# Reading two PSUM banks with ScalarE alone, and adding the parts with GpSimd

## The chip, the cores and the metric

The kernel runs on one core of a Trainium2 chip. The metric is the time of one execution on the device in microseconds (us). Five engines work side by side, each through its own queue in order: TensorE (PE; its weight loads are listed as PEld), VectorE (DVE), ScalarE (ACT), GpSimd (POOL) and SyncE (SP), which here issues nearly all DMAs. Matmuls write to PSUM, eight banks of 128 partitions by 512 floats; the other engines copy results from there to SBUF.

## The reference

A gated sum of two branches over an input x of 2048 rows and 640 columns:

```python
g = sigmoid((x * gate_w).sum(-1, keepdims=True))
a = attention(x, wqkv) @ wo          # 32 heads of 20 columns, softmax over 2048 keys
fa = x @ dft_hid_re.T;  fb = x @ dft_hid_im.T          # DFT over the features
b = dft_seq_re @ fa - dft_seq_im @ fb                  # real part of the DFT over the rows
return g * a + (1 - g) * b
```

All of it is in float32. Matmuls that need that precision split each operand into a leading part and a rest and add three products.

## The kernel before

The first 270 us project queries, keys and values, and make 10 of 64 tiles of the feature DFT. From then on the attention runs in 256 *cycles* of four *steps*; step i is one of 1024 pairs of score tiles of the second pass. In each cycle TensorE computes eight score tiles for the row maxima (kind "m", read by VectorE, L170) and eight for the exponentials (kind "e", read by ScalarE, L832), and between them a share of the other branch (kind "F", fill). At the end stands "B", `burst`: 16 matmuls of probabilities and values (L494). The order is written out by hand as a string of 16 scores, the fills and the burst:

```python
ORDER = "emFemFFFFemFeFFmeFFemFFFmmFFmeeB"
```

Cycle c begins the steps 4c+1 to 4c+4, one with every second "e" (`begin(i)`, `end(i)`). `at_step(i, fn)` lets `begin(i)` call `fn`; this sets the place of a DMA in SyncE's queue and of an operation in its engine's queue, while the time follows from semaphores. `extras` holds read-outs and adds with the step from which they may run; `run_extras`, called in `burst` ahead of its matmuls, takes up to two of them.

Score tiles rotate over five PSUM banks (`ps`), the values' sum holds one (`av`), and two banks, `yp0` and `yp1`, take the fill. A fill tile is computed in halves: rows 0 to 63 of both operands go to `yp0`, rows 64 to 127 to `yp1`, and the result is the sum of the two banks. The fills are, in order:

- 54 feature tiles (`hid_tile`, matmuls at L346), one per cycle, until 605 us. Tile c ends with the last fill of cycle c, at step 4c+3; its banks are read at the end of that cycle: ScalarE copies `yp0` to a `raw` buffer with its sign (L354), VectorE adds `yp1` (L355). The store to `a_scr` in HBM is put at step now+2, which is 4c+5.
- the DFT over the rows (`dft_step`, L575), until 1688 us, read in the same way (L594, L595); the change does not touch it.
- 30 output tiles (`out_tile`, L646), one per cycle. ScalarE copies `yp0` times the gate to a tile `m` (L655), VectorE adds `yp1` times the gate (L658). In the last 41 steps VectorE does both (L657, L658). GpSimd scales the other branch's row and adds `m` (L662, L663).

The `raw` buffers (`raw_tile`, three of 128x1024 floats) are shared. In the feature stage they serve each tile, from its read-out until its store has landed, and the loads that are split by GpSimd afterwards: `load_wb` (the next 128x966 and 128x644 weights, in cycles 6 and 22) and `load_c` (two 128x1024 pieces of the row DFT, in cycles 47, 49 and 51; GpSimd adds the two at L465 and splits the sum at L112 and L113). Both take two `raw` buffers when `end(4c+2)` calls them, and are split from step 4c+4 or 4c+6 on. GpSimd also multiplies the attention's output by the reciprocal sums (L524). A tile that takes a buffer waits until the buffer's last user is done with it. SyncE's other transfers in this stage are the queries' and keys' rows of the next pair of heads (L785), the rows of maxima (L210, L211, put two steps behind a `burst`), and the sums' way through HBM (L508 to L532).

Of the kernel before, what the change touches and what calls it, by code (L numbers as in the profile page):

```python
# [10 lines left out]
F32 = mybir.dt.float32  # L11
R = mybir.dt.float32r
AF = mybir.ActivationFunctionType
ALU = mybir.AluOpType
# [4 lines left out]
P = 128  # L19
# [7 lines left out]
HE = D // 2  # L27
# [40 lines left out]
def f32(ap):  # L68
    return ap.bitcast(F32)
# [3 lines left out]
def mix_kernel(ctx: ExitStack, tc: tile.TileContext, xa, wqk, wb, cdft, wo, out):  # L73
    nc = tc.nc
    pe, act, dve, pool, sp = nc.tensor, nc.scalar, nc.vector, nc.gpsimd, nc.sync
# [15 lines left out]
    a_scr = dram.tile([2, 2, NS, P, HE], F32, name="a_scr")  # L91
# [36 lines left out]
    def raw_tile():  # L128
        return work.tile([P, 1024], F32, name="raw", bufs=3)
# [22 lines left out]
    now, later = [-1], {}  # L152

    def at_step(i, fn):
        later.setdefault(i, []).append(fn)
# [38 lines left out]
    def new_y(z):  # L194
        yp[z] = ps_y.tile([P, 512], F32, name=f"yp{z}")
        return yp[z]
# [139 lines left out]
    def hid_tile(i, read_out):  # L336
        j, st = divmod(i, NS)
        hf, ri = divmod(j, 2)
        new_y(0), new_y(1)
        w = wt["b", 2 + j]  # L340
        cs = slice(st * P, (st + 1) * P)
        for d in range(ND):
            for z, (xz, wz) in enumerate(((0, 0), (0, 1), (1, 0))):
                for h in range(2):
                    r = slice(64 * h, 64 * h + 64)
                    pe.matmul(yp[h][:, :HE], xs[r, xz, d, cs], w[r, wz, d, :HE],  # L346
                              start=d == 0 and z == 0, stop=d == ND - 1 and z == 2)
                if (d, z) != (ND - 1, 2):
                    yield
        a = raw_tile()[:, :HE]  # L350
        y0, y1 = yp[0][:, :HE], yp[1][:, :HE]

        def read():
            act.activation(a, y0, AF.Copy, scale=-1.0 if ri else 1.0)  # L354
            dve.tensor_tensor(a, a, y1, op=ALU.subtract if ri else ALU.add)  # L355

        read_out(read, (a_scr[ri, hf, st], a))
        yield


    def segment(i, steps):
        def read_out(read, args):
            read()
            stores.append(args)

        tile_ = hid_tile(i, read_out)
        left = 3 * ND
        for k in range(steps):
            run_s(step + 1)
            for _ in range(left // (steps - k)):  # L370
                next(tile_)
                left -= 1
# [3 lines left out]
    def run_s(upto):  # L376
        nonlocal step
        while step < upto:
            s_step(step)
            step += 1  # L380
# [37 lines left out]
    for n, c in enumerate(order):  # L418
        for t in range(4):
            m = 4 * n + t  # L420
# [24 lines left out]
    def a_tile(n, s):  # L445
        at[n, s] = apool[0].tile([P, 2, HE], R, name=f"a{n}_{s}")
        return at[n, s]
# [97 lines left out]
    st = {(th * HT + t, hf): 0 for th in range(2) for t in range(HT) for hf in range(2)}  # L545
# [4 lines left out]
    outs, extras, made = {}, [], {}  # L550
# [83 lines left out]
    def out_tile(tt, hf):  # L634
        new_y(0), new_y(1)
        if hf == 0:
            k = tt - PRE[0]
            yo[tt] = f32(a_tile(1, 2 * ND + k) if 2 * ND + k < NS else a_tile(0, k)).rearrange("p z c -> p (z c)")
            assert all(st[tt, h] == 0 for h in range(2))
            sp.dma_start(yo[tt], y_scr[tt])  # L640
        o = opre[tt]
        for d in range(ND - 1):
            for z, (oz, wz) in enumerate(((0, 0), (0, 1), (1, 0))):
                for h in range(2):
                    r = slice(64 * h, 64 * h + 64)
                    pe.matmul(yp[h][:, :HE], o[r, oz, d], wos[d, hf][r, wz], start=d == 0 and z == 0, stop=d == ND - 2 and z == 2)  # L646
                if (d, z) != (ND - 2, 2):
                    yield
        m = apool[0].tile([P, HE], F32, name="m", bufs=2)
        y0, y1 = yp[0][:, :HE], yp[1][:, :HE]  # L650
        g = gate[:, tt : tt + 1]

        def read():
            if now[0] < total - LEAD:
                act.activation(m, y0, AF.Copy, scale=g)  # L655
            else:
                dve.tensor_scalar(m, y0, g, 1.0, op0=ALU.mult, op1=ALU.mult)  # L657
            dve.scalar_tensor_tensor(m, y1, g, m, op0=ALU.mult, op1=ALU.add)  # L658

        def add():  # L660
            y = yo[tt][:, hf * HE : (hf + 1) * HE]
            pool.tensor_scalar(y, y, ngate[:, tt : tt + 1], float(signs[tt, hf]), op0=ALU.mult, op1=ALU.mult)  # L662
            pool.tensor_tensor(y, y, m, op=ALU.add)  # L663

        extras.append((now[0], read))
        extras.append((now[0] + 3, add))
        yield

# [33 lines left out]
    apool = []  # L702
# [28 lines left out]
    LAST = {total - 10: load_o4, total - 9: load_old, total - 8: lambda: fins.append(load_o(0)), total - 2: lambda: fins.pop()()}  # L731
    done = 0
    goals, fins = {}, []
    def read_later(read, args):
        extras.append((now[0], read))
        at_step(now[0] + 2, functools.partial(sp.dma_start, *args))

    HID = 4 * NS - HEAD
    fills = itertools.chain(*(hid_tile(HEAD + g, read_later) for g in range(HID)), itertools.chain.from_iterable(dft_step(g) for g in range(NS * UNITS)),
                            itertools.chain.from_iterable(out_tile(tt, hf) for tt in PRE for hf in range(2)))  # L740


# [238 lines left out]
```

## Time and profile before

| | |
|---|---|
| time, median of 3 runs | 1891.77 us (1891.42 to 1894.12) |
| span of the profiled execution, first to last instruction | 1888.5 us |
| the execution's own time beside its span | not shown by the profile; the runs' median is 3.3 us above the span |
| granted TensorE clock, mean | 1.000 |
| HBM traffic over the span | 147 GB/s |
| TensorE: row DFT (L575), feature DFT (L346), output (L646) matmuls | 649.1, 236.0, 89.5 us |
| VectorE: maxima (L170) | 1294.8 us, 2048 of 684 ns |
| ScalarE: exponentials (L832) | 1087.0 us, 2048 of 599 ns |

A row of a group or a waiting list gives engine, line, operation, result and operands, and the count; a timeline row begins with the start and the duration in us, and ends, in brackets, with the time that the engine had been idle and what released it. A row of a window gives the busy time of PE, PEld, DVE, ACT and POOL in it with the number of instructions, the granted clock, the DMA engines' busy share and the GB/s moved.

### The profile page before, as it was taken

To read this page: it belongs to the slowest core of one execution; us is meant where nothing else is said; L and a number is where in the kernel's file an instruction comes from. 1 tells how busy PE (TensorE), PEld (TensorE's weight loads), DVE (VectorE), ACT (ScalarE), POOL (GpSimd) and SP (SyncE) were. 2 spreads that over 40 slices of the span, in tenths; PEclk is the share of its full clock that TensorE was granted. 3 is DMA by queue.
4 is the path that set the end of the run, shared out by engine and by line. 5 is a ranking of instruction groups with operands and counts; after the bars stand their busy time and mean duration, and the time that the engine had idled before them with its cause. 6 is when DMAs were issued, how large, how long until landed. Compare 5 with 4: busy or idle time off the path is not lost. (4 is left out here: it accounts for less than half of the span.)

```text
span 1888.5 us, 44537 instructions
## 1 busy us (share of the span) xinstructions
PE 1877.4 (99%) x17453; PEld 1358.2 (72%) x17453; DVE 1470.0 (78%) x2445; ACT 1219.1 (65%) x2350; POOL 1005.1 (53%) x872
## 2 busy tenths in 40 slices
PE   9999999999999999999999999999999999999998
PEld 8987777777776677776767677776767677766666
DVE  4145569989898888888888888888888888889954
ACT  4221147777777767666767667666767676677785
POOL 1200001010004999466699989958879988734343
PEclk9999999999999999999999999999999999999999
DMA  7843341221215575536557576736475746442214
GB/s 232 181 133 128 128 154 48 62 76 49 75 58 147 163 238 178 148 123 169 180 176 238 171 234 190 201 119 189 156 220 195 225 147 205 154 114 70 62 49 157
DMA packets 174804, 280.50 MB, mean 149 GB/s; under 512 B 44303, under 2 KB 106895, under 8 KB 174595
## 3 DMA queue, kind: packets, MB, share of 16 engines
q1 hardware_dynamic: 173635, 275.70, 47.7%
q0 software_dynamic: 960, 1.97, 0.6%
q8 instruction: 137, 2.24, 0.5%
q14 instruction: 72, 0.59, 0.1%
HBM read 213.37 MB, written 63.52 MB: 147 GB/s over the span
## 5 line engine op out<-in xcount | busy, mean ns | idle before, releaser
L170 DVE TENSOR_REDUCE mx<-ps 128x1 f32<-128x512 f32 x2048 | 1294.8, 684 | 175.8 <-PE ps L168 154.8
L832 ACT ACTIVATE p<-ps 128x512 f32<-128x512 f32 x2048 | 1087.0, 599 | 432.7 <-PE ps L168 223.6
L168 PE MATMUL ps<-kst,qst 60*128 60x512 f32 x2048 | 785.2, 415 | 3.7 <-DVE mx L170 1.7
L830 PE MATMUL ps<-qst,kst 62*128 62x512 f32 x2048 | 698.9, 413 | 0.5 <-ACT p L832 0.3
L575 PE MATMUL yp<-a,part 64*128 64x320 f32 x5376 | 649.1, 307 | 0.0
L575 PEld LDWEIGHTS yp<-a,part 64*128 64x128 f32 x5376 | 582.2, 186 | 7.3
L494 PE MATMUL av<-p,v 128*21 128x512 f32 x4096 | 491.3, 596 | 0.0
L830 PEld LDWEIGHTS ps<-qst,kst 62*128 62x128 f32 x2048 | 335.7, 185 | 200.9 <-DVE mx L170 182.4
L168 PEld LDWEIGHTS ps<-kst,qst 60*128 60x128 f32 x2048 | 371.2, 184 | 24.7 <-DVE mx L170 9.6
L113 POOL TENSOR_TENSOR part<-raw,part 128x1024 fp32r<-128x1024 f32 (+1 forms) x129 | 290.4, 2251 | 10.3
L494 PEld LDWEIGHTS av<-p,v 128*21 128x21 f32 x4096 | 98.4, 100 | 226.7 <-issue 223.2
L346 PE MATMUL yp<-wb,xs 64*128 64x320 f32 x1920 | 236.0, 308 | 0.1
L112 POOL CAST part<-raw 128x1024 fp32r<-128x1024 f32 (+1 forms) x129 | 127.0, 985 | 161.5 <-PE yp L575 141.2
L346 PEld LDWEIGHTS yp<-wb,xs 64*128 64x128 f32 x1920 | 206.0, 186 | 4.5 <-DVE raw L355 0.5
L465 POOL TENSOR_TENSOR raw<-raw,raw 128x1024 f32<-128x1024 f32 x77 | 185.4, 2408 | 6.4 <-DMA raw<-in_cdft 4.8
L112 POOL CAST wb<-raw 128x966 fp32r<-128x966 f32 (+1 forms) x4 | 3.4, 862 | 255.4 <-DMA raw<-in_wb 255.4
L524 POOL TENSOR_TENSOR o<-o,rb 128x512 f32<-128x512 f32 x31 | 40.2, 1296 | 146.6 <-DMA rb<-r_scr 100.8
L113 POOL TENSOR_TENSOR a<-araw,a 128x320 fp32r<-128x320 f32 x112 | 97.6, 872 | 9.0
L113 DVE TENSOR_TENSOR p<-ps,p 128x512 fp32r<-128x512 f32 x40 | 27.5, 691 | 93.5 <-ACT p L110 90.8
L646 PE MATMUL yp<-a,part 64*128 64x320 f32 x720 | 89.5, 309 | 0.0
L110 ACT ACTIVATE p<-ps 128x512 fp32r<-128x512 f32 x40 | 23.7, 597 | 100.6 <-PE ps L118 100.6
L646 PEld LDWEIGHTS yp<-a,part 64*128 64x128 f32 x720 | 76.9, 186 | 2.5
(86 smaller groups left out, 1237.0 us busy)
## 6 DMA issues: line engine op xcount, KB each, us to landing
raw<-in_cdft SPq DMA_DIRECT2D x192, 512.0 KB
araw<-a_scr SPq DMA_DIRECT2D x192, 160.0 KB
qk_scr<-p SPq DMA_DIRECT2D x40, 512.0 KB
kst<-qk_scr SPq DMA_DIRECT2D x90, 160.0 KB
qst<-qk_scr SPq DMA_DIRECT2D x90, 160.0 KB
a_scr<-raw SPq DMA_DIRECT2D x64, 160.0 KB
yt<-y_scr SPq DMA_DIRECT2D x64, 160.0 KB
y_scr<-yt SPq DMA_DIRECT2D x64, 160.0 KB
```

What stands on the lines that cost most here:

```text
L112: e1.tensor_copy(dst1, src)
L113: e2.tensor_tensor(dst2, src, f32(dst1), op=ALU.subtract)
L168: pe.matmul(ps, q[b : b + KROWS, qt * P : (qt + 1) * P], k[b : b + KROWS, kc * 512 : (kc + 1) * 512], start=True, stop=True)
L170: return lambda: dve.tensor_reduce(mx[n][:, h, qt, kc : kc + 1], ps, axis=AX.X, op=ALU.max)
L346: pe.matmul(yp[h][:, :HE], xs[r, xz, d, cs], w[r, wz, d, :HE], start=d == 0 and z == 0, stop=d == ND - 1 and z == 2)
L465: pool.tensor_tensor(raws[0], raws[0], raws[1], op=ALU.add if PRODUCTS[n][0][1][0] > 0 else ALU.subtract)
L494: pe.matmul(av[32 * j : 32 * j + DH + 1, :], v[:, kt, h * (DH + 1) : (h + 1) * (DH + 1)], pp[qc][:, h, :], start=kt == 0, stop=kt == NS - 1)
L524: pool.tensor_tensor(o, o, rb, op=ALU.mult)
L575: pe.matmul(yp[h][:, :HE], c[r, cz, cs], a[r, az], start=s == 0 and z == 0, stop=s == NS - 1 and z == 2)
L646: pe.matmul(yp[h][:, :HE], o[r, oz, d], wos[d, hf][r, wz], start=d == 0 and z == 0, stop=d == ND - 2 and z == 2)
L830: pe.matmul(pt, k[b : b + KROWS + 2, kt * P : (kt + 1) * P], q[b : b + KROWS + 2, qc * 512 : (qc + 1) * 512], start=True, stop=True)
L832: act.activation(pts[n, kt, qc][:, h], pt, AF.Exp, scale=float(DH) ** -0.5)
```

## The change

For feature tiles made within the attention, and for output tiles up to the last 41 steps, ScalarE reads both banks, each into memory of its own, and VectorE no longer takes part. For a feature tile the second part goes to the other half of the same `raw` buffer; at step now+2 GpSimd adds the two in SBUF, and the store stands at step now+4. For an output tile the second part goes to a new tile `m2` with one buffer, and GpSimd adds both parts to the row, one after the other. The ten feature tiles made ahead of the attention, the row DFT's tiles and the last output tiles are read as before.

```diff
-        a = raw_tile()[:, :HE]
+        raw = raw_tile()
+        a, b = raw[:, :HE], raw[:, HE : 2 * HE]
         y0, y1 = yp[0][:, :HE], yp[1][:, :HE]
 
-        def read():
+        def read(alone):
             act.activation(a, y0, AF.Copy, scale=-1.0 if ri else 1.0)
-            dve.tensor_tensor(a, a, y1, op=ALU.subtract if ri else ALU.add)
-
-        read_out(read, (a_scr[ri, hf, st], a))
+            if alone:
+                act.activation(b, y1, AF.Copy, scale=-1.0 if ri else 1.0)
+            else:
+                dve.tensor_tensor(a, a, y1, op=ALU.subtract if ri else ALU.add)
+
+        def add():
+            pool.tensor_tensor(a, a, b, op=ALU.add)
+
+        read_out(read, add, (a_scr[ri, hf, st], a))
         yield
...
     def segment(i, steps):
-        def read_out(read, args):
-            read()
+        def read_out(read, add, args):
+            read(False)
             stores.append(args)
...
         g = gate[:, tt : tt + 1]
+        parts = [m]
 
         def read():
             if now[0] < total - LEAD:
+                parts.append(apool[0].tile([P, HE], F32, name="m2"))
                 act.activation(m, y0, AF.Copy, scale=g)
+                act.activation(parts[1], y1, AF.Copy, scale=g)
             else:
                 dve.tensor_scalar(m, y0, g, 1.0, op0=ALU.mult, op1=ALU.mult)
-            dve.scalar_tensor_tensor(m, y1, g, m, op0=ALU.mult, op1=ALU.add)
+                dve.scalar_tensor_tensor(m, y1, g, m, op0=ALU.mult, op1=ALU.add)
 
         def add():
             y = yo[tt][:, hf * HE : (hf + 1) * HE]
             pool.tensor_scalar(y, y, ngate[:, tt : tt + 1], float(signs[tt, hf]), op0=ALU.mult, op1=ALU.mult)
-            pool.tensor_tensor(y, y, m, op=ALU.add)
+            for part in parts:
+                pool.tensor_tensor(y, y, part, op=ALU.add)
...
-    def read_later(read, args):
-        extras.append((now[0], read))
-        at_step(now[0] + 2, functools.partial(sp.dma_start, *args))
+    def read_later(read, add, args):
+        extras.append((now[0], functools.partial(read, True)))
+        at_step(now[0] + 2, add)
+        at_step(now[0] + 4, functools.partial(sp.dma_start, *args))
```

## The prediction

> **What bounds the kernel now.** I read the page's engine shares first, then the timelines of one cycle in each stage of the attention, then SyncE's queue around the loads that share the `raw` buffers.
>
> ```profile
> span 1888.5 us, 44537 instructions
> PE 1877.4 (99%) x17453; PEld 1358.2 (72%) x17453; DVE 1470.0 (78%) x2445; ACT 1219.1 (65%) x2350; POOL 1005.1 (53%) x872
> ```
>
> TensorE has no idle time to speak of, so another engine's work counts only where TensorE waits for it. The change touches two stages: 54 feature tiles, one per cycle, and 20 of the 30 output tiles. The first and last start of their ScalarE reads give the cycle lengths.
>
> ```profile
> L354 ACT ACTIVATE raw<-yp x54: 437/443/445, 270.6 to 604.6; 128x320 f32<-128x320 f32 x54
> L655 ACT ACTIVATE m<-yp,gate x20: 532/532/532, 1693.6 to 1810.1; 128x320 f32<-128x320 f32 x20
> ```
>
> So a feature cycle takes (604.6 - 270.6)/53 = 6.30 us, an output cycle (1810.1 - 1693.6)/19 = 6.13 us. Now the read-out in one feature cycle (the end of cycle 6, rows of three engines):
>
> ```profile
> 308.22 0.44 ACT L354 ACTIVATE raw<-yp 128x320 f32<-128x320 f32 x1
> 309.62 1.82 ACT L832 ACTIVATE p<-ps 128x512 f32<-128x512 f32 x3 [0.96 <-PE ps L168]
> 308.69 0.49 DVE L355 TENSOR_TENSOR raw<-raw,yp 128x320 f32<-128x320 f32 x1 [0.20 <-ACT raw L354]
> 309.59 0.69 DVE L170 TENSOR_REDUCE mx<-ps 128x1 f32<-128x512 f32 x1 [0.41 <-PE ps L168]
> 309.36 0.32 PE L346 MATMUL yp<-wb,xs 64*128 64x320 f32 x2
> ```
>
> The read-out lies under the attention-value burst. After it both engines still wait for TensorE's next scores (0.96 us, 0.41 us), and the next tile's first matmuls come at 309.36, after VectorE is done at 309.18. Next, a cycle just after the feature stage, which has no read-out at all (two VectorE rows), and an output cycle:
>
> ```profile
> 612.26 4.97 DVE L170 TENSOR_REDUCE mx<-ps 128x1 f32<-128x512 f32 x8 [1.10 <-PE ps L168]
> 618.34 4.40 DVE L170 TENSOR_REDUCE mx<-ps 128x1 f32<-128x512 f32 x7 [1.11 <-PE ps L168]
> ...
> 1736.58 0.53 ACT L655 ACTIVATE m<-yp,gate 128x320 f32<-128x320 f32 x1
> 1738.01 3.12 ACT L832 ACTIVATE p<-ps 128x512 f32<-128x512 f32 x6 [0.90 <-PE ps L168]
> 1737.15 0.55 DVE L658 SCALAR_TENSOR_TENSOR m<-yp,gate,m 128x320 f32<-128x320 f32 x1 [0.26 <-ACT m L655]
> 1737.99 5.00 DVE L170 TENSOR_REDUCE mx<-ps 128x1 f32<-128x512 f32 x8 [0.29 <-PE ps L168]
> 1737.85 0.88 POOL L663 TENSOR_TENSOR a<-a,m 128x320 f32<-128x320 f32 x1 [2.80 <-DVE m L658]
> ```
>
> Without any read-out the cycle is 618.34 - 612.26 = 6.08 us, about the output cycle's 6.13. What times an output cycle is the loop maxima, last scores, burst, next scores; VectorE's 0.55 us fills a hole in it and is followed by 0.29 us of waiting.
>
> **The change, part by part.**
>
> *VectorE loses* 54 x 0.49 us and 20 x 0.55 us. In both stages its next maximum waits for TensorE after the read-out, so the path gains 0. The far end: feature cycles fall to the 6.08 us of a cycle without read-out, 54 x 0.22 = 12 us; but they carry more matmuls than that one, and VectorE's 0.41 us of waiting says that it is not what they wait for. I take 0.
>
> *ScalarE gains* 54 x 0.44 us and 20 x 0.53 us. Feature cycle: the second read runs from 308.66 to about 309.1 where the next exponential starts at 309.62, and frees the second bank before VectorE does now (309.18). Output cycle: from 1737.11 to 1737.64, against 1738.01. Covered by 0.96 and 0.90 us of waiting; without that cover 24 + 11 = 35 us. I take 0.
>
> *GpSimd gains* 54 adds of about 0.87 us (the size of L663) and 20 more in the output tiles. There it starts on the first part at about 1737.25 rather than 1737.85 and is done near 1739.0, four microseconds before the next second read may overwrite `m2`, which has a single buffer. Cost 0. In the feature stage GpSimd is mostly idle.
>
> *The store of a feature tile moves* from step now+2 to now+4 in SyncE's queue, and the add takes its place at now+2 in GpSimd's. With three `raw` buffers this is the part that can reach the path. Twice a load of new weights (`load_wb`, cycles 6 and 22) and three times one of DFT rows (`load_c`, cycles 47, 49, 51) takes two of the three buffers at the end of step 4c+2. The tile of the same cycle must then take the third one: that of the tile before. Its store was at 4c+1, ahead of the load. Now it is at 4c+3, behind it. So ScalarE's read of tile c waits until a store has landed that was issued behind 0.8 to 1 MB of loads; behind that read stand all later exponentials, and TensorE's next `yp` matmuls wait for the banks.
>
> Cycle 6, in SyncE's waits, its timeline, and the windows of the DMA:
>
> ```profile
> SPq L785 <- DVE raw L355: 238.5, 53, 5.9
> ...
> 302.75 0.31 SPq L785 DMA_DIRECT2D a_scr<-raw  x1
> 306.08 0.86 SPq L278 DMA_DIRECT2D raw<-in_wb  x2
> ...
> 310.00:311.00 1.00, 1.00 (x16) 0.98 (x14) 1.00 (x3) 0.87 (x3) 0.91 (x2) 1.00 0.50 170
> 311.00:312.00 1.00, 1.00 (x15) 0.98 (x13) 0.99 (x2) 1.00 (x3) 1.00 (x1) 1.00 0.01 3
> ```
>
> SyncE stands and waits for nearly every store (53 times, 238.5 us), so the order in its queue is the order of issue. Tile 5's store now goes at 302.75, 3.3 us ahead of the loads; changed, it goes after 306.94. The loads keep the DMA busy to about 310.6 (share 0.50 of 310 to 311, then 0.01). At 170 / 0.50 = 340 GB/s the 160 KB of the store add 0.5 us: it lands at 311.1. Tile 6's read, at 308.22 now, starts 2.9 us late; TensorE's first `yp` pair, at 309.36 now, gets its second bank 0.85 us after the read starts, at 311.95: **2.6 us** lost. Bounds: 0, if the store is served beside the loads, and 3.
>
> Cycle 22, the same rows:
>
> ```profile
> 406.69 1.96 SPq L278 DMA_DIRECT2D raw<-in_wb  x2
> 408.69 1.82 SPq L521 DMA_DIRECT2D rb<-r_scr  x4
> 408.87 0.44 ACT L354 ACTIVATE raw<-yp 128x320 f32<-128x320 f32 x1
> 412.00:413.00 1.00, 1.00 (x16) 0.99 (x14) 0.94 (x3) 1.00 (x4) 1.00 (x1) 1.00 0.72 227
> 413.00:414.00 1.00, 1.00 (x13) 0.82 (x9) 1.00 (x2) 0.55 (x2) 1.00 (x2) 1.00 0.01 3
> ```
>
> The loads are issued until 408.65, and the DMA is busy to about 412.7 with them and what follows. Tile 21's store comes directly behind the loads: it lands near 412.8, against a read at 408.87. By the same steps 3.9 us late, **3.6 us** lost; bounds 0 and 4.
>
> The three loads of DFT rows, in SyncE's, ScalarE's and GpSimd's timelines:
>
> ```profile
> 561.30 2.31 SPq L459 DMA_DIRECT2D raw<-in_cdft  x2
> 566.16 0.44 ACT L354 ACTIVATE raw<-yp 128x320 f32<-128x320 f32 x1
> 567.77 2.39 POOL L465 TENSOR_TENSOR raw<-raw 128x1024 f32<-128x1024 f32 x1 [53.85 <-DVE raw L355]
> 573.69 1.29 POOL L524 TENSOR_TENSOR o<-o,rb 128x512 f32<-128x512 f32 x1
> 575.73 0.86 SPq L459 DMA_DIRECT2D raw<-in_cdft  x2
> 579.04 0.44 ACT L354 ACTIVATE raw<-yp 128x320 f32<-128x320 f32 x1
> 583.43 2.38 POOL L465 TENSOR_TENSOR raw<-raw 128x1024 f32<-128x1024 f32 x1 [8.46 <-DMA raw<-in_cdft]
> 585.85 0.44 ACT L354 ACTIVATE raw<-yp 128x320 f32<-128x320 f32 x1 [0.45 <-POOL raw L465]
> 589.72 1.20 SPq L459 DMA_DIRECT2D raw<-in_cdft  x2
> 592.01 0.44 ACT L354 ACTIVATE raw<-yp 128x320 f32<-128x320 f32 x1
> 595.53 2.39 POOL L465 TENSOR_TENSOR raw<-raw 128x1024 f32<-128x1024 f32 x1 [6.14 <-DMA raw<-in_cdft]
> ```
>
> GpSimd's sum (L465) starts when the megabyte has landed, 5.8 to 7.7 us after the first issue. By cycle 6 a read that is d late costs d - 0.3. Cycle 47: SyncE no longer waits for tile 46's store first, on average 238.5 / 53 = 4.5 us a store; if a third of that, 1.5 us, moves the load ahead, it has landed by 566.3 and the store by 566.8, 0.6 us after the read was due: **0.3 us** (0 to 1.5). Cycle 49: GpSimd's split ends with L524's start at 573.69, which frees a buffer; the load, no longer behind a store, goes out at about 574.2 and lands 5.8 us later, the store at 580.5 (its add stands behind L524 and ends near 576, in time), 1.4 us after the read was due: **1.1 us** (0 to 3). Cycle 50: GpSimd's sum, which held this read 0.45 us, is earlier: **-0.4 us**. Cycle 51: with the load where it is, tile 50's store lands at 595.9, 3.9 us after 592.01, and costs 3.6 us; if SyncE, not waiting for the store, issues the load two microseconds sooner, 1.4 us. I take **2.5 us**.
>
> Sum: 2.6 + 3.6 + 0.3 + 1.1 - 0.4 + 2.5 = 9.7 us. The span becomes 1898.2 us. What lies around it is taken as the 3.3 us between the span of 1888.5 and the runs' median of 1891.77; the forecast is 1891.8 + 9.7 = 1901.5 us.
>
> The order of landing decides this. The Trainium skill, "DMA: Bandwidth & Descriptors", section "Queues, rings and completion order", says that each DMA engine takes its descriptors in ring order but that completion is not first-in first-out over a queue, since a later short transfer may sit on fewer engines. By its first half the sum stands; if its second half held for these stores, the sum would be near 0. The DMA windows show no gap in which a 160 KB store could slip past the loads, and the store uses 128 rows as the loads do, so I go with the first.
>
> **Rivals.**
>
> *The stores land in time* (they overtake, or the loads move up everywhere). For it: SyncE has slack once it no longer waits 238.5 us for stores. Against it: before cycle 6's load stand the rows of maxima, which SyncE cannot issue before the transpose, so that load cannot move up. Time: 1891.8 - 0.4, about 1891.4 us.
>
> *Faster: VectorE is the bound of the feature cycles.* Freed of 0.49 us, they would fall from 6.30 towards 6.08 us: 54 x 0.22 = 12 us, 1880 us. It decides where VectorE's next maximum follows its read-out without a wait; the 0.41 us before it speak against that. In the output cycles there is only 6.13 - 6.08 to win, 1 us in 20.
>
> *ScalarE becomes the bound.* If a second read delays the exponentials by 0.2 us in each of 74 cycles, +15 us on 1891.8: 1907 us. It decides where the 0.4 to 0.5 us that the second read leaves free are used up; the rows leave them.
>
> *The clock drops after the stalls.* Three waits of TensorE of 2.5 us or more are new; every window shows a granted clock of 1.00 today. Were each followed by half a cycle at half speed, 3 x 3.15 us would come on top: 1911 us. The Trainium skill, "TensorE: Matmul & The Clock Gate", Part 1, states such a rule: about 3.4 us without work halve the clock until about 3.4 us of work have passed. No row here shows it.
>
> **How the numbers follow.** Forecast 0.75, stores in time 0.11, faster 0.04, ScalarE 0.05, clock 0.05. The median of three runs lies within 0.2% of another, 3.8 us, which I take as what can be told apart. Faster 0.04; same 0.11; slower 0.85, the rest. The forecast's own range, from its bounds, is 1895 to 1905 us; to leave out no more than two in ten I go from 1892 to 1907.
>
> **What would show it.** Right: in the list of waits ScalarE's feature read waits for a store (`a_scr<-raw`), two to four times, of 2 to 4 us, at cycles 6, 22 and 51; TensorE shows holes of that size there; the other feature cycles and the output cycles keep their length. Wrong: no such waits, or shorter output cycles, or exponentials that start later in every cycle.

## The result, and the profile after

The changed kernel takes 1905.08 us (median of four, 1902.72 to 1908.4) against 1892.94 us of the kernel before on the same chip (four, 1891.42 to 1894.68): a ratio of 1.0065, 95% interval 1.0051 to 1.0079, some 12 us slower. The forecast was 1901.5 us, slower. The profiled execution has a span of 1902.6 us, 14.1 us above the one before.

The page of the kernel after (span, busy time by engine, and the group of GpSimd's new adds) shows that the work moved as the diff says: VectorE lost 38 us, ScalarE gained 27, GpSimd 64.

```profile
span 1902.6 us, 44617 instructions
PE 1884.4 (99%) x17453; PEld 1360.4 (72%) x17453; DVE 1432.3 (75%) x2371; ACT 1246.5 (66%) x2424; POOL 1069.2 (56%) x946
...
L362 POOL TENSOR_TENSOR raw<-raw 128x320 f32<-128x320 f32 x54 | 47.1, 872 | 418.5 <-ACT raw L357 205.1
```

The list of waits after has a row that the kernel before has not. Behind the colon stand the total, the number and the longest: ScalarE's feature read waits three times for a store to land.

```profile
ACT raw L355 <- DMA a_scr<-raw: 9.2, 3, 3.2
```

SyncE's timeline after, around the first and the third of them, shows the new order: the store of the tile before (L797) stands behind a pair of loads.

```profile
308.27 1.00 SPq L278 DMA_DIRECT2D raw<-in_wb  x2
309.32 0.42 SPq L797 DMA_DIRECT2D a_scr<-raw  x1
...
581.42 3.16 SPq L466 DMA_DIRECT2D raw<-in_cdft  x2
586.33 0.33 SPq L797 DMA_DIRECT2D a_scr<-raw  x1
...
601.61 0.33 SPq L797 DMA_DIRECT2D a_scr<-raw  x1
```

ScalarE's timeline after has the reads that waited for them (L355), and at the end the one of cycle 51, which did not wait:

```profile
313.41 0.44 ACT L355 ACTIVATE raw<-yp 128x320 f32<-128x320 f32 x1 [2.87 <-DMA a_scr<-raw]
...
418.26 0.44 ACT L355 ACTIVATE raw<-yp 128x320 f32<-128x320 f32 x1 [3.11 <-DMA a_scr<-raw]
592.38 0.44 ACT L355 ACTIVATE raw<-yp 128x320 f32<-128x320 f32 x1 [3.20 <-DMA a_scr<-raw]
...
606.06 0.45 ACT L355 ACTIVATE raw<-yp 128x320 f32<-128x320 f32 x1
```

The first store was issued by 309.74 and the read began at 313.41: 3.7 us behind 0.8 MB of loads (128 x 966 and 128 x 644 floats). TensorE's feature matmuls wait for that read in turn. Its timeline after has a hole, that is idle time, of 2.16, 2.41 and 2.50 us at the same places, 7.1 us in all:

```profile
313.90 0.74 PE L346 MATMUL yp<-wb,xs 64*128 64x320 f32 x2 [2.16 <-ACT raw L355]
418.75 0.74 PE L346 MATMUL yp<-wb,xs 64*128 64x320 f32 x2 [2.41 <-ACT raw L355]
592.87 0.74 PE L346 MATMUL yp<-wb,xs 64*128 64x320 f32 x2 [2.50 <-ACT raw L355]
```

What a hole costs is more than its length. Windows from one burst to the next, which I call a cycle by its number, first those of the kernel before: the ones that begin with bursts 6, 22, 49 and 50, then the 20 output cycles, and a stretch of 3.41 us ahead of the attention's regular cycles.

```profile
307.18:313.45 6.27, 6.27 (x64) 4.45 (x63) 5.62 (x11) 4.57 (x9) 3.61 (x3) 1.00 0.46 155
407.83:414.10 6.27, 6.27 (x65) 4.48 (x63) 5.60 (x11) 4.57 (x9) 3.47 (x3) 1.00 0.69 196
577.99:584.24 6.25, 6.25 (x64) 4.45 (x63) 5.58 (x10) 4.57 (x9) 0.81 (x1) 1.00 0.80 245
584.24:591.00 6.76, 6.65 (x65) 4.64 (x63) 5.66 (x10) 4.86 (x9) 5.01 (x3) 1.00 0.70 160
1686.46:1809.13 122.67, 122.67 (x1124) 82.22 (x1122) 112.02 (x190) 93.39 (x183) 48.71 (x62) 1.00 0.26 72
266.96:270.37 3.41, 3.41 (x38) 2.41 (x38) 3.40 (x6) 2.82 (x6) 0.00 (x0) 1.00 0.63 159
```

The same windows of the kernel after, with two stretches from within the cycle of burst 6 behind its row:

```profile
309.38:319.88 10.50, 8.34 (x64) 6.11 (x63) 5.26 (x9) 5.22 (x10) 6.05 (x5) 0.84 0.32 107
313.90:314.75 0.85, 0.85 (x7) 0.70 (x9) 0.00 (x0) 0.76 (x2) 0.85 (x1) 1.00 0.00 0
314.75:318.16 3.41, 3.41 (x26) 3.41 (x25) 1.89 (x3) 1.84 (x4) 3.33 (x4) 0.50 0.00 0
414.00:424.65 10.65, 8.24 (x64) 6.04 (x62) 5.51 (x10) 5.24 (x10) 6.06 (x5) 0.84 0.37 131
588.02:598.78 10.76, 8.27 (x64) 6.05 (x62) 5.47 (x10) 5.24 (x10) 5.36 (x4) 0.84 0.57 161
598.78:605.02 6.24, 6.24 (x64) 4.38 (x63) 4.96 (x8) 4.90 (x10) 2.13 (x2) 1.00 0.60 206
1699.50:1822.08 122.58, 122.58 (x1129) 80.98 (x1125) 101.23 (x170) 101.71 (x203) 64.17 (x80) 1.00 0.28 76
266.96:270.37 3.41, 3.41 (x26) 3.23 (x24) 2.02 (x4) 1.81 (x4) 0.00 (x0) 0.50 0.84 214
```

Three cycles are 4.23, 4.38 and 4.51 us longer, 13.1 us together. Of each, some 2.2 to 2.5 us is the hole; and although the matmuls are the same, TensorE is busy for 2 us more (8.34 against 6.27). That is the clock: 0.85 us after it resumes, its granted clock falls to 0.50 for a window of 3.41 us, in which it does 1.71 us of work. Three holes (7.1 us), three such windows (5.1 us) and 0.9 us that I do not divide further make the 13.1. The cycle of burst 50 is 0.52 us shorter, the other feature cycles up to burst 51 together 0.8 us shorter, the output cycles unchanged (122.58 against 122.67 us for twenty).

The remaining 2.2 us are there by burst 6 (309.38 against 307.18), and already by burst 0 (271.73 against 269.49), ahead of the first read that the change touches; 1.7 us of them are the half-clock window in the last rows. The same stretch has it or not in profiles of kernels with the same code there (the run with only the output tiles changed has it, the run with only the store moved has not), so it may be part of the 3 us by which runs of one kernel differ. So the profile's 14.1 us fit the runs' 12 us.

### The profile page after: what moved, and what is told of

Its sections match the earlier page's. It is cut to its first block, busy times and chain, and to the rows that moved or that the text cites. A ratio compares the mean times of both kernels' runs of the same rounds, so it can differ in the third digit from the quotient of the medians.

```text
span 1902.6 us, 44617 instructions
## 1 busy us (share of the span) xinstructions
PE 1884.4 (99%) x17453; PEld 1360.4 (72%) x17453; DVE 1432.3 (75%) x2371; ACT 1246.5 (66%) x2424; POOL 1069.2 (56%) x946
## 5 line engine op out<-in xcount | busy, mean ns | idle before, releaser
L362 POOL TENSOR_TENSOR raw<-raw 128x320 f32<-128x320 f32 x54 | 47.1, 872 | 418.5 <-ACT raw L357 205.1
L346 PE MATMUL yp<-wb,xs 64*128 64x320 f32 x1920 | 241.7, 314 | 7.1 <-ACT raw L355 7.1
L472 POOL TENSOR_TENSOR raw<-raw,raw 128x1024 f32<-128x1024 f32 x77 | 185.5, 2409 | 5.4 <-DMA raw<-in_cdft 5.0
L674 POOL TENSOR_TENSOR a<-a,m 128x320 f32<-128x320 f32 x50 | 43.5, 871 | 70.6 <-ACT m L664 54.6
```

The source lines that it names most:

```text
L362: pool.tensor_tensor(a, a, b, op=ALU.add)
L472: pool.tensor_tensor(raws[0], raws[0], raws[1], op=ALU.add if PRODUCTS[n][0][1][0] > 0 else ALU.subtract)
```

## The experiments

Two theories stood at the start. A: the order of the stores and the loads that share the three `raw` buffers makes the whole loss. B: the moved work itself (ScalarE's second read, GpSimd's adds) makes part or all of it. Each run was timed beside the kernel before, and "expected" is what was written ahead of it.

**The changed kernel, with the store back at step now+2**, behind the add:

```diff
-        at_step(now[0] + 4, functools.partial(sp.dma_start, *args))
+        at_step(now[0] + 2, functools.partial(sp.dma_start, *args))
```

> The changed kernel, with the store of a feature tile back at step now+2, behind the add. The store stands ahead of the loads again, but still waits for GpSimd's add. Theory A (only the store's place behind a load costs): no wait of ScalarE's feature read for a store, cycles 6, 22 and 49 at 6.2 to 6.3 us, a time of 1890 to 1893 us. Rival B (the work moved to ScalarE and GpSimd costs by itself, or the store is late because the add takes 0.87 us on GpSimd): the three long cycles stay, in whole or in part, and the time is 1897 to 1905 us.

1895.75 us, ratio 1.0020 (1.0010 to 1.0030). The cycles of bursts 6, 22 and 49 are back at 6.22 to 6.27 us, and ScalarE never waits for a store. But one long cycle is left, that of burst 50. In this kernel's list of waits ScalarE's read waits once, for GpSimd's sum:

```profile
ACT raw L355 <- POOL raw L472: 2.9, 1, 2.9
```

GpSimd's timeline, with tile 48's add (L362) and that sum (L472):

```profile
575.55 1.28 POOL L531 TENSOR_TENSOR o<-o,rb 128x512 f32<-128x512 f32 x1
576.79 0.87 POOL L362 TENSOR_TENSOR raw<-raw 128x320 f32<-128x320 f32 x1
...
587.20 2.35 POOL L472 TENSOR_TENSOR raw<-raw 128x1024 f32<-128x1024 f32 x1 [5.12 <-DMA lc<-l_scr]
```

SyncE's timeline, with the tile's store and the load of the two pieces:

```profile
577.69 0.34 SPq L797 DMA_DIRECT2D a_scr<-raw  x1
...
579.88 0.90 SPq L466 DMA_DIRECT2D raw<-in_cdft  x2
```

The window of the cycle:

```profile
585.48:595.90 10.42, 8.17 (x64) 6.08 (x63) 5.24 (x9) 5.21 (x10) 6.59 (x4) 0.84 0.57 140
```

Tile 48's add stands on GpSimd behind the multiplication L531 and ends at 577.66; the store waits for it, and with it all that SyncE has queued behind, down to the load at 579.88, which went at 575.73 in the kernel before; this kernel is 1.3 us behind there, so 2.9 us of that count. GpSimd's sum of the two loaded pieces therefore starts at 587.20 (583.43 before), and ScalarE's read, which needs the buffer that this sum frees, waits 2.93 us instead of 0.45. So A holds for the three long cycles, and B in one place: not by the duration of an add, but by one add that a store waits for.

**The kernel before, with only the store moved**, no work moved between engines:

```diff
-        at_step(now[0] + 2, functools.partial(sp.dma_start, *args))
+        at_step(now[0] + 4, functools.partial(sp.dma_start, *args))
```

> The kernel before, with nothing but the store of a feature tile moved from step now+2 to now+4; VectorE still adds the second bank. Theory A: the long cycles appear without any work moved between engines, at cycles 6, 22 and one of 49 or 51, each 4 to 4.5 us longer, about 1903 to 1906 us. Rival B: no long cycles, 1891 to 1894 us.

1907.46 us, ratio 1.0081 (1.0068 to 1.0095): the moved store alone makes the whole loss, and rather more than the whole change. The list of waits, and ScalarE's read of cycle 49:

```profile
ACT raw L354 <- DMA a_scr<-raw: 8.3, 3, 4.5
...
ACT raw L354 <- POOL raw L465: 2.5, 1, 2.5
...
593.78 0.44 ACT L354 ACTIVATE raw<-yp 128x320 f32<-128x320 f32 x1 [2.53 <-POOL raw L465]
```

The windows of bursts 6, 22 and 49:

```profile
307.35:319.41 12.06, 9.57 (x64) 7.29 (x62) 5.85 (x11) 4.91 (x9) 5.22 (x4) 0.72 0.31 96
413.74:426.02 12.28, 8.40 (x65) 6.12 (x63) 5.64 (x10) 4.91 (x9) 6.45 (x5) 0.86 0.38 113
590.09:600.44 10.35, 8.40 (x64) 6.11 (x62) 5.65 (x10) 4.90 (x9) 5.76 (x3) 0.84 0.71 207
```

The same three cycles are long. In cycles 6 and 22 the read waits for a store, as in the change (3.19 and 4.47 us); the third wait for a store, of 0.67 us, is in cycle 47. In cycle 49 the wait that ends last is the one for GpSimd's sum of the pieces just loaded, so this run shows that the store's place makes the loss there too, but not that the store's landing does. The first two cycles lose 5.8 and 6.0 us rather than 4.2 and 4.4. In the first that is mostly a second window at half clock (TensorE busy for 9.57 us, clock 0.72), in the second a longer hole (12.28 - 8.40 = 3.88 us); why that read waits longer was not settled.

**The kernel before, with only the output tiles changed** as in the diff (`m2`, the second ScalarE read, two adds by GpSimd):

> Only the output tiles as in the change; feature tiles as before. Theory A: output cycles of 6.10 us as before and no long cycle, 1891.5 to 1894 us. Rival B: the second read and the second add delay 20 cycles by 0.1 us or more, 1895 us or above; if VectorE had been the bound there, below 1889 us.

1893.56 us, ratio 1.0002 (0.9994 to 1.0011): nothing, in either direction. VectorE's 20 x 0.55 us were not on the path, and ScalarE's 20 x 0.53 us are covered.

**The changed kernel, with the weight loads called one step later**, behind the tile's store instead of ahead of it:

```diff
-        if i % 4 == 2:
+        if i % 4 == 3:
             ...
-                at_step(i + 2, load_wb(3 + (c + HEAD) // NS, pool, pool))
+                at_step(i + 1, load_wb(3 + (c + HEAD) // NS, pool, pool))
+        if i % 4 == 2:
+            c = i // 4
```

> The changed kernel, with the two loads of weights (cycles 6 and 22) taken one step later in the program, behind the store of the tile before; the loads of DFT rows stay ahead of it. Theory A: the long cycles 6 and 22 fall to 6.25 us, the one at 49 stays: 4.2 + 4.4 us less than the changed kernel, about 1896.5 us. Rival B: as the changed kernel, 1905 us.

1896.59 us, ratio 1.0025 (1.0016 to 1.0035), two thirds of the loss gone. The time came as expected, but its parts did not. The list of waits:

```profile
ACT raw L355 <- DMA a_scr<-raw: 5.1, 3, 2.1
```

SyncE's timeline at cycle 22:

```profile
407.88 0.38 SPq L797 DMA_DIRECT2D a_scr<-raw  x1
408.36 1.92 SPq L278 DMA_DIRECT2D raw<-in_wb  x2
```

The windows of bursts 22, 49 and 51:

```profile
408.99:416.20 7.21, 6.80 (x65) 4.63 (x63) 5.25 (x9) 5.08 (x10) 3.68 (x3) 1.00 0.55 164
579.52:587.47 7.95, 6.81 (x64) 4.63 (x62) 5.26 (x9) 5.09 (x10) 3.99 (x3) 1.00 0.70 189
593.71:601.94 8.23, 6.79 (x65) 4.62 (x63) 5.36 (x10) 5.08 (x10) 3.98 (x3) 1.00 0.22 81
```

The loads now follow the store, and ScalarE no longer waits in cycle 6. Cycle 22 keeps a wait of 1.13 us though its store goes ahead of the loads; the transfers of the row maxima stand ahead of that store in SyncE's queue, and whether it is they was not tried. Cycles 49 and 51, whose loads were left alone, lose 1.7 and 2.0 us, with holes of 1.1 and 1.4 us, instead of 4.5 us in one. No hole here halves the clock.

**The changed kernel, with only the second piece of each weight load behind the store**, the first piece ahead of it as in the change:

```diff
+            load(0, 3)
+            at_step(i + 1, functools.partial(load, 3, ND - 3))
...
-                at_step(i + 2, load_wb(3 + (c + HEAD) // NS, pool, pool))
+                at_step(i + 2, load_wb_apart(3 + (c + HEAD) // NS, i))
```

> The changed kernel, with only the second piece of each weight load (128x644, cycles 6 and 22) moved behind the store of the tile before; the first piece (128x966) stays ahead of it, and so do the loads of DFT rows. Theory A (a store lands behind what was issued before it, and TensorE's hole follows from that): the two reads wait about 1 us less than in the changed kernel, the holes of TensorE at cycles 6 and 22 shrink from 2.2 to 2.8 us to about 1.3 to 1.8 us, and with holes that short the clock does not fall there: cycles 6 and 22 of 7.6 to 8.1 us and a time of about 1905.1 - 2 x 2.7 = 1899.7 us. Rival C (what counts is that the store's buffer is shared with the loads, not the order of landing): cycles 6 and 22 keep 10.5 us, 1905 us. Rival D (the store does not wait for the bytes ahead of it): cycles of 6.3 us, 1896.5 us.

1902.19 us, ratio 1.0049 (1.0034 to 1.0065). The read of cycle 6 waits 2.23 us instead of 2.87: less data ahead of the store, less waiting. The windows of bursts 6 and 22:

```profile
308.07:317.93 9.86, 8.33 (x65) 6.12 (x63) 5.25 (x9) 5.25 (x10) 6.08 (x5) 0.83 0.30 97
412.05:420.59 8.54, 6.80 (x65) 4.62 (x63) 5.25 (x9) 5.10 (x10) 5.19 (x4) 1.00 0.50 144
```

Both holes have the size expected (9.86 - 8.33 = 1.53, and 8.54 - 6.80 = 1.74 us), yet the time was missed by 2.5 us: the hole of 1.53 us lowered the clock, the one of 1.74 us did not. What decides between them has to be something else than length alone; the last section comes back to it.

**The changed kernel, with the store back at now+2 and VectorE's add back from cycle 46 on**: the first experiment without the add that held SyncE up.

```diff
+        alone = now[0] < 4 * 46
-        extras.append((now[0], functools.partial(read, True)))
-        at_step(now[0] + 2, add)
-        at_step(now[0] + 4, functools.partial(sp.dma_start, *args))
+        extras.append((now[0], functools.partial(read, alone)))
+        if alone:
+            at_step(now[0] + 2, add)
+        at_step(now[0] + 2, functools.partial(sp.dma_start, *args))
```

> The changed kernel with the store back at step now+2, and with VectorE adding the second bank, as before the change, in the eight feature tiles from cycle 46 on. Theory A' (what the store's place leaves over is the add's place in GpSimd's queue around the loads of DFT rows): the long cycle at burst 50 goes back from 10.4 to 6.8 us, no cycle of the feature stage over 7 us, 1891 to 1893 us, not to be told from the kernel before. Rival B (moved work costs in every cycle): above 1894 us.

1892.03 us against 1892.68, ratio 0.9996 (0.9987 to 1.0005): not to be told from the kernel before. ScalarE waits neither for a store nor for GpSimd's sum. 46 feature tiles and 20 output tiles without VectorE thus neither cost nor win anything that these runs can tell. No version here is shown faster than the kernel before.

**The changed kernel, with only the load of cycle 49 put behind the store** (called at the end of step 4c+3), to see what becomes of cycle 51, where the forecast had a loss and the change has none:

```diff
-            if c in (HID - 7, HID - 5, HID - 3):
+            if c in (HID - 7, HID - 3):
...
+        if i == 4 * (HID - 5) + 3:
+            at_step(i + 3, load_c(1))
```

> The changed kernel, with only the second load of DFT rows (cycle 49) taken one step later, behind the store of tile 48; the weight loads (6, 22) and the other DFT rows (47, 51) stay ahead of their stores. Theory A (each load ahead of a store makes its own wait; cycle 51 was spared in the changed kernel only because the wait at 49 had put TensorE 4.5 us behind the DMA): the cycles after bursts 6 and 22 stay near 10.5 us, the wait for a store leaves cycle 49; at 50 the read waits about 3 us for GpSimd's sum, as with the store put back; and at 51, where load and store keep the changed kernel's order, a wait for a store of 1 to 4 us appears. Rival G (the loads of DFT rows share one delay, which the order at 49 alone makes): no wait at 51.

1905.18 us in one run. ScalarE's timeline has the read of cycle 51:

```profile
602.89 0.44 ACT L355 ACTIVATE raw<-yp 128x320 f32<-128x320 f32 x1 [3.68 <-DMA a_scr<-raw]
```

The windows of bursts 49 and 51:

```profile
585.60:591.82 6.22, 6.22 (x65) 4.28 (x63) 5.07 (x9) 4.90 (x10) 2.37 (x2) 1.00 0.79 249
...
598.05:610.20 12.15, 9.17 (x64) 7.02 (x62) 5.53 (x11) 5.24 (x10) 6.27 (x4) 0.72 0.30 98
```

With cycle 49 whole, the wait comes up in cycle 51, as A has it: 3.68 us for a store behind loads, with a hole in TensorE of 12.15 - 9.17 = 2.98 us. In the change it was absent, by this account, because TensorE had already lost its time in cycle 49, so that the store had landed when the read was due: the load of cycle 51 went out 6.0 us ahead of the read there (600.07 against 606.06), here 2.9 us ahead of the time at which the read was due (596.32 against 599.21). The wait for GpSimd's sum that was expected in cycle 50 did not come.

**The kernel before, with 6, 9, 12, 15, 18 or 21 more ScalarE copies ahead of the feature read** in the even cycles from 8 to 42, a ladder of holes to measure the clock by itself. The copies go to a tile that nobody reads:

```diff
+    scr = const.tile([P, P], F32, name="scr")
...
+            if 8 <= c < 44 and c % 2 == 0:
+                for _ in range((6, 9, 12, 15, 18, 21)[(c - 8) // 2 % 6]):
+                    act.activation(scr, ident, AF.Copy)
```

> The kernel before, with 6, 9, 12, 15, 18 or 21 copies of a 128x128 tile put on ScalarE ahead of the feature read of every second cycle from 8 to 42, three times each; they change no result and only delay the read, so that TensorE gets a hole of known length. Theory E (the clock is halved for 3.41 us after a hole of more than about 2 us): cycles with holes up to 1.7 us are longer by the hole alone, those with holes of 2.2 us or more by the hole and 1.7 us. Rival F (the clock falls at random times, or by the sum of many holes): half-clock windows do not follow the longer holes.

The first two rungs in TensorE's timeline:

```profile
325.31 0.93 PE L347 MATMUL yp<-wb,xs 64*128 64x320 f32 x2 [1.06 <-ACT raw L360]
340.88 0.93 PE L347 MATMUL yp<-wb,xs 64*128 64x320 f32 x2 [2.10 <-ACT raw L360]
```

Windows around the first rung (cycle 8) and the second (cycle 10):

```profile
321.90:330.00 8.10, 6.93 (x67) 4.62 (x69) 5.68 (x11) 6.50 (x16) 0.00 (x0) 1.00 0.06 22
336.40:347.00 10.60, 8.38 (x64) 6.12 (x62) 5.62 (x10) 7.53 (x18) 0.00 (x0) 0.84 0.04 15
```

Holes of 1.06 to 1.13 us left the clock at 1.00 (three of three) and lengthened the cycle by 1.8 us; holes of 2.1, 3.2, 4.2, 5.2 and 6.2 us lowered it every time (15 of 15), for one or two windows of 3.4 us. At 2.1 us the cycle is 4.4 us longer (4.1 and 5.5 us in the other two): the size of each loss in the change, made without any store or load.

## Why the prediction was right, and where its terms were off

*The mechanism* was the one forecast: a store put behind loads that share its buffers, a ScalarE read that waits for it, a hole in TensorE. Moving the store alone makes the loss, moving it back takes all three waits for a store away.

*Cycle 6*: the read was put 2.9 us late and was 2.87. The cost was put at 2.6 us and is 4.23. The hole of 2.16 us is within that; the 1.7 us of the halved clock were not in the sum.

*Cycle 22*: 3.9 us late forecast, 3.11 measured; the store landed sooner than the end of DMA traffic suggested. Cost 3.6 forecast, 4.38 measured: a hole 1.2 us smaller than that, and the clock.

*Cycle 49* was the term that was most off: 1.1 forecast, 4.51 measured. GpSimd's timeline after has the add of tile 48:

```profile
585.43 0.87 POOL L362 TENSOR_TENSOR raw<-raw 128x320 f32<-128x320 f32 x1
```

The changed kernel is 10.03 us behind there (burst 49 at 588.02 instead of 577.99). With that taken off, the load's second piece was issued by 574.55, where the forecast had 574.2, and the add ended at 576.27: "ends near 576, in time" came true. The step that failed is the landing "5.8 us later". The store went out at 586.33, behind the add and with transfers of the queries' and keys' rows around it, and the read could start at 592.38, 3.20 us late instead of 1.4. In the kernel before, this very load took 7.7 us from its issue to the start of GpSimd's sum (575.73 to 583.43 in the prediction's rows); the forecast took the shortest of its three, 5.8 us. With 7.7 us its own sum gives 3.3 us late. The 1.7 us of the clock came on top here too.

*Cycle 51*: 2.5 forecast, nothing measured. The term was right by itself (the run with cycle 49 whole shows 3.68 us of waiting there), but the sum added terms that are not independent: the wait in 49 puts TensorE back against SyncE's queue, and the read at 606.06 finds a store that was issued at 601.61. (The lower price in this term, 1.4 us, should be 1.6 by the forecast's own rule: 1.9 us late, less 0.3.)

*Cycles 47 and 50*: 0.3 forecast and no wait found; -0.4 forecast, -0.52 measured.

*The work between the engines* was put at 0, and the run with output tiles alone and the run with VectorE from cycle 46 bear that out; neither ScalarE nor VectorE became the bound. The one exception is not in the change as made: with the store behind the add in the same step, the add holds SyncE's queue up.

*The clock* was a rival with a chance of 0.05, as a loss of 3.15 us for each wait on top of the forecast. It came as mechanism and not as size: 1.7 us a wait, 5.1 us in all. By the trace, the sum of the holes alone is 7.1 us, less than the 9.7 forecast; the clock brought it above. The forecast of 1901.5 was thus near in part by luck, for errors that partly cancel: too much for the holes, with cycle 51 in them, and nothing for the clock. The measured 1905.08 lies just past the 1895 to 1905 us that its own bounds gave. The Trainium skill, "TensorE: Matmul & The Clock Gate", Part 1, has the clock fall after an idle window of about 3.4 us, free-running. The windows of 3.41 us agree with the rows; that a whole idle window is needed does not: holes of 2.1 us were enough each time, and one of 1.53 us was.

*The order of landing*: the Trainium skill, "DMA: Bandwidth & Descriptors", section "Queues, rings and completion order", has descriptors consumed in ring order on each DMA engine. The stores behind the loads agree: none overtook in the three cycles in question, where the reads that needed their buffers waited 2.87, 3.11 and 3.20 us.

## What to carry to other kernels

A DMA that is moved a step later is judged by what it is moved past: look for every load in between that takes a buffer from the same pool, and for the reader that will then need the buffer of the moved store. A hole in TensorE costs more than its length: here one of 2.2 to 2.5 us cost its length and 2 us more, 1.7 us of them by the clock, and one of 1.1 us cost 1.7 to 1.9 us, without the clock. Where two waits hang on the same queue, price the second one with the first already in place, since the delay of the first may have hidden it.

## What was unexpected of the hardware

The granted clock halves after much shorter holes than I had taken, and always for whole windows of 3.41 us. Every hole of 2.0 us or more had it, in these kernels; of those between 1.5 and 1.9 us some had and some had not (1.53 and 1.83 did, 1.74 did not); none of up to 1.44 us behind a read did.

The traces show more of the rule than the length. Within a run, the falls of the clock begin a whole number of windows apart (in the run with only the store moved at 311.85, 421.08 and 595.16 us: 32 and 51 windows of 3.413 us), so the windows lie on a fixed grid. What sorts the holes behind reads is the idle time that falls into one window at full clock: with 1.60 us or more a half-clock window followed each time, with up to 1.29 us never, and in between 1.53 us had one and 1.59 us had not. The hole of 1.53 us lay in a single window; that of 1.74 us lay across two, with 0.98 and 0.76 us. A second half-clock window followed where 0.32 us or more of the hole reached into the first, and not where it was 0.06 us or less.

Yet idle time is not the whole rule. Ahead of the attention's cycles, near 263 us, a hole of half a microsecond in a stretch with few matmuls was followed by such a window in some profiles (the last rows of the windows above) and not in others. Where the feature tiles end, the run with one load behind the store has one at 622.80 us and the run with only the output tiles changed one at 612.13 us, each behind a stretch of few matmuls (3.2 and 3.5 a us, where a feature cycle has 10) and with no hole over 0.02 us in TensorE's rows there. While TensorE has work, a fall of the clock costs half of its window.
